# Attention with a relative-position bias, then a mixture of adapters: the bias of half the key tiles moved onto TensorE, the gating onto VectorE, slots and beginning reordered

## The chip, the cores and the metric

The kernel runs on one core of a Trainium2 chip. The metric is the device time of one execution in microseconds. A core has TensorE (PE in the profile; PEld are its weight loads), VectorE (DVE), ScalarE (ACT), GpSimd (POOL), and SyncE (SP), which here only issues DMAs. Each engine works through its own instructions in order and waits on semaphores for the others. PE writes to PSUM alone; DVE and ACT read PSUM.

## What is computed

```python
B, H, S, D = 8, 8, 576, 64                       # q, k, v: (B, H, S, D), float32
scores = q @ k.transpose(0, 1, 3, 2) / sqrt(D)
bias = bias_table[bucket(abs(i - j))]            # 32 buckets, one value per head
attn = softmax(scores + bias)
x = (attn @ v)                                   # as (B * S, H * D) = (4608, 512)

logits = x @ w_gate                              # 8 experts
w = softmax over the two largest logits of a row
out = x + sum over these two of w_e * (x @ A[e]) @ B[e]     # rank 16
```

The bias depends on the distance alone, and from a distance of 128 on it is one value. A value that all keys share cancels in the softmax, so the kernel takes it off the table first: what is left is zero beyond 127.

## The kernel before

**Units and slots.** A unit is one pair of heads of one batch: 32 units, four a batch. A unit has six slots (`SLOTS`). Scores are computed transposed, keys on the partitions and queries along the free dimension. The 512 first keys are four key tiles of 128; their scores are 4 x 576 columns a head, cut in slots of 512 columns: slots 0 to 3 are 2 x 512 columns, slot 4 is 2 x 256. Slot 5 has the 64 last keys (tile 4), the two heads on the two halves of the partitions. In `scores` PE fills one of two score buffers (`sc`, PSUM), and ACT's exp reads it and writes the probabilities in bfloat16: `pm` for the four key tiles (L311), `pe` for the last keys (L319). The two heads stand on partitions 0-63 and 64-127 of `qkT`, so their score matmuls use the two halves of PE's rows.

**Bias.** exp(s + b) = exp(s) exp(b): after the exp DVE multiplies the band of queries within 128 of a key tile by a table of exp(bias) (`bias`): tile 0 in one instruction (512 elements a partition), tiles 1 and 2 together (1536), tile 3 (640), and the last keys (192, L325). The table `eb` is a row of 512 values a head that every partition reads one element further on; the row is computed by DVE and ACT (`table_row`), written to DRAM (`gx_d`), and loaded from there with overlapping rows (`table_load`).

**Values.** In `values` and `whole` PE multiplies the probabilities of a unit by v and a column of ones (L362, 90 matmuls of 65 columns a unit, accumulated in `pv`). This comes one unit later. `normalise` divides by the row sum (L394, L395) and writes `xn`.

**Inputs.** SP loads q, k and v of a batch in pieces of a head, nearly two batches ahead. POOL casts them to bfloat16 (L149, L153), PE transposes q and k (L275), DVE copies them out of PSUM (L279).

**Adapters.** When a batch is done, its tiles of 128 rows are taken in groups of two or three (`Group`): transposes of x, the matmul with A and w_gate together (`zl`), the gates, the product of gate and z (`zt`), its transpose, the matmul with B (`dl`), and the sum with x (L482). A weight softmax over two logits is (1 + tanh)/2. These steps stand in `queue`; `step_pe` takes the next step's PE part, `step_dve` runs what belongs to it on the other engines a little later. `enqueue` interleaves the second half of one group with the first half of the next. z is copied out of PSUM by ACT (L441); of the gates DVE does the maximum and the mask, POOL six small operations and `zt` (L455 to L462), ACT the tanh (L458). The factor 1/2 is in `Bc`, which ACT makes from moe_B (L249) in unit 4. The last batch has a routine of its own (`Last`).

**Order.** The order on each engine is the order of the program: a loop over 192 slots, in which `if s == ...` says what follows the scores of each slot. The PSUM pool `mp` has two buffers (tag `mm`) for everything but scores and `pv`, so a third PE step waits until the first has been copied out. The lines of the slots:

```python
if s == 0: bias(p, 3); finish(p - 1); step_pe()
if s == 1: bias(p, 4); cast_v(u + 1); step_dve(); step_pe()
if s == 2: values(p, 0, 0, 1, 2, 3, 4); cast_qk(u + 2, 0); step_dve()
if s == 3: transpose_pe(u + 1); bias(u, 0); step_pe()
if s == 4: cast_qk(u + 2, 1); transpose_out(u + 1); step_dve()
if s == 5: values(p, 1, 0, 1, 2, 3); bias(u, 1, 2)
```

This is the middle of the kernel; `p` is the unit before `u`, and the last four units (`late`) take values, finish and bias earlier.

Of the kernel before, what the change touches and what calls it, by code (L numbers as in the profile page):

```python
# [33 lines left out]
def kernel(  # L34
# [23 lines left out]
    TE = 192  # L58
# [30 lines left out]
    def load(b):  # L89
# [14 lines left out]

        def tail_qk(*engs):
            for i, (src, eng) in enumerate(zip((q, k), engs)):
                todo.append(lambda i=i, src=src, eng=eng: eng.dma_start(
                    out=qke32[i * 64:(i + 1) * 64],
                    in_=src[b, :, 512:, :].rearrange("h p d -> p h d")))
# [7 lines left out]
        for hp in range(HP if b else 0):  # L117
            main(nc.sync, q32, q, hp)
            main(nc.sync, k32, k, hp)
            if hp == 0:  # L120
                tail_qk(nc.sync, nc.sync)
            main(nc.sync, v32, v, hp)
            if hp == 0:
                tail_v()
        if b == 0:
            main(nc.sync, q32, q, 0)
            main(nc.scalar, k32, k, 0)
            tail_qk(nc.sync, nc.scalar)
            main(nc.sync, q32, q, 1)
            main(nc.sync, k32, k, 1)  # L130
            main(nc.sync, v32, v, 0)
            tail_v()
            todo.append(lambda: table_load(0))
            for hp in range(2, HP + 1):
                if hp < HP:
                    main(nc.sync, q32, q, hp)
                    main(nc.sync, k32, k, hp)
                todo.append(lambda hp=hp: table_load(hp - 1))
                main(nc.sync, v32, v, hp - 1)
        return deque(todo)  # L140
# [26 lines left out]
    nc.sync.dma_start(out=btT, in_=bias_table.rearrange("b h -> h b"))  # L167
    gx = cp.tile([H, GW], FP32, tag="gx")
    gxe = cp.tile([H, GW], BF16, tag="gxe")
    gx_d = nc.dram_tensor("gx_d", (H, GW), BF16, kind="Internal")  # L170
# [3 lines left out]
    ebe = cp.tile([128, HP, TE], BF16, tag="ebe")  # L174

    def table_row():
        nc.vector.memset(gx, 0.0)
# [13 lines left out]
        nc.scalar.activation(gxe, gx, ACT.Exp)  # L191
        nc.scalar.dma_start(out=g, in_=gxe)

    def table_load(hp):
        nc.sync.dma_start(
            out=eb[:, 2 * hp:2 * hp + 2, :],
            in_=bass.AP(tensor=g.tensor, offset=g.offset + 2 * hp * GW,
                        ap=[[1, 128], [GW, 2], [1, TW]]))
        if hp == 0:
            for par in range(2):  # L200
                nc.sync.dma_start(
                    out=ebe[par * 64:(par + 1) * 64, :, :],
                    in_=bass.AP(tensor=g.tensor, offset=g.offset + par * GW + TW - TE,
                                ap=[[1, 64], [2 * GW, HP], [1, TE]]))

# [4 lines left out]
    todo = load(0)  # L210
    for i in range(6):
        todo.popleft()()
    table_row()
    while todo:
        todo.popleft()()
    spread = cp.tile([128, 4, 128, 4], BF16, tag="spread")
    nc.vector.memset(spread, 0.0)
    for c in range(4):
        nc.gpsimd.tensor_copy(out=spread[:, c, :, c], in_=ident)
# [21 lines left out]
    def cast_adapters(i):  # L241
# [4 lines left out]
        elif i == 1:  # L246
            nc.gpsimd.tensor_copy(out=A4[:, :, ER:], in_=Gf)
        else:
            nc.scalar.mul(Bc, Bf, 0.5)  # L249

    def order_adapters(i):
        ps = mp.tile([128, 2, ER + E], FP32, name="Ap", tag="mm")
        for k in range(2):
            for c in range(4):
                lhsT = spread[:, c].rearrange("p m f -> p (m f)")
                nc.tensor.matmul(ps[:, k, :],
                                 lhsT=lhsT[:, (2 * i + k) * 128:(2 * i + k + 1) * 128],
                                 rhs=A4[:, c, :], start=(c == 0 and k == 0), stop=(c == 3),
                                 skip_group_check=True)
        nc.vector.tensor_copy(AW[:, 2 * i:2 * i + 2, :], ps)  # L260
# [15 lines left out]

    def transpose_out(u):
# [9 lines left out]
    def tails_out(b):  # L287
        nc.vector.tensor_copy(batch_tiles(b)[:, :, :, 512:],
                              tps.pop("e").rearrange("p g (i t) -> p g i t", i=2))

    def scores(u, s):
# [7 lines left out]
        if s < SLOTS - 1:  # L299
            c, end = SW * s, min(SW * (s + 1), 4 * S)  # L300
            n = end - c
            while c < end:
                j, q0 = divmod(c, S)
                w = min(S - q0, end - c)
                for h in range(2):
                    rows = slice(h * 64, (h + 1) * 64)
                    nc.tensor.matmul(sc[:, h, c - SW * s:c - SW * s + w],  # L307
                                     lhsT=kT[rows, j * 128:(j + 1) * 128],
                                     rhs=qT[rows, q0:q0 + w], start=True, stop=True)
                c += w  # L310
            nc.scalar.activation(pm[:, :, SW * s:end], sc[:, :, :n], ACT.Exp, scale=scale)  # L311
        else:
            flat = sc.rearrange("p a b -> p (a b)")
            for q0, n in ((0, 512), (512, 64)):
                for h in range(2):
                    rows = slice(h * 64, (h + 1) * 64)
                    nc.tensor.matmul(flat[rows, q0:q0 + n], lhsT=kT[rows, 512:],  # L317
                                     rhs=qT[rows, q0:q0 + n], start=True, stop=True)
            nc.scalar.activation(pe, flat[:, :S], ACT.Exp, scale=scale)  # L319

    def bias(u, j, n=1):
        b, hp = units[u]
        pm, pe = probs[u]
        if j == 4:
            nc.vector.tensor_tensor(pe[:, S - TE:], pe[:, S - TE:],  # L325
                                    _ap(ebe, hp * TE + TE - 1, [[-1, TE]]), op=ALU.mult)
            return
        q0, q1 = max(0, (j - 1) * 128), min(S, (j + 2) * 128)
        e0 = 2 * hp * TW + TW - 1 - (q0 - (j - 1) * 128)
        w = q1 - q0  # L330
        if n == 1:
            t, e = pm[:, :, j * S + q0:j * S + q1], _ap(eb, e0, [[TW, 2], [-1, w]])
        else:
            t = _ap(pm, j * S + q0, [[4 * S, 2], [S + 128, n], [1, w]])
            e = _ap(eb, e0, [[TW, 2], [0, n], [-1, w]])
# [74 lines left out]
    state = {"now": None, "last": None}  # L410
# [385 lines left out]
```

## Time and profile before

| | us |
|---|---|
| three runs | 232.77, 234.53, 236.08 |
| median | 234.53 |
| the profiled execution, whole | 232.95 |
| its span, first to last instruction | 230.8 |

| engine | busy us | share of the span | instructions |
|---|---|---|---|
| PE | 171.1 | 74% | 4138 |
| DVE | 172.0 | 75% | 381 |
| ACT | 173.0 | 75% | 228 |
| POOL | 104.5 | 45% | 202 |

Busy time counts an engine's own instructions; those that only wait, or issue a DMA, are not in it. A group of instructions is shown as: line, engine, operation, out<-in by the program's names, partitions x elements and type, how many | busy time, mean ns of one | idle time of the engine just before them, and what ended most of it. Matmuls overlap, so their mean is longer than the time that each adds. In a view by windows each row is one stretch of the span: its length, then for each engine busy time and number of instructions, the clock that the throttle granted PE, the share of time in which the DMA engines were busy, and GB/s. A line of waits is: who waited <- for whom: us in total, how many times, the longest. A line of the timeline is: start, length, engine, line, operation, names, shape, how many, and in brackets the idle time before it and what ended it.

### The profile page before, as it was taken

The numbers are of one execution on the slowest core, as the hardware profiler recorded it, in microseconds if no ns is written. First come the engines' busy times: TensorE is split into PE (matmuls) and PEld (weight loads), VectorE is DVE, ScalarE is ACT, GpSimd is POOL, SyncE is SP. The second block draws the span as 40 slices with busy tenths as digits, with TensorE's granted clock in tenths as the row PEclk, the third lists the DMA queues.
The fourth block names the chain that finished last, engine by engine and source line by source line (L and its number), as shares of the span: only waits on it lengthen the run. The fifth ranks groups of instructions, "written<-read, shape, count | busy, mean of one in ns | idle before, by whom it ended". The sixth has DMA issues, their size and how long they took to land.

```text
span 230.8 us, 9744 instructions
## 1 busy us (share of the span) xinstructions
PE 171.1 (74%) x4138; PEld 117.4 (51%) x4156; DVE 172.0 (75%) x381; ACT 173.0 (75%) x228; POOL 104.5 (45%) x202
## 2 busy tenths in 40 slices
PE   0477876298586998979578889788879885866741
PEld 0235645175354665646346656566556654653620
DVE  4342577166588889999888899999999978984760
ACT  3186779378679979989598979999889975884422
POOL 1422553630797019296394075666456626312010
PEclk9999999779979999999999999999999999997985
DMA  7989989998886888789889867897779504123106
GB/s 139 177 183 224 215 168 206 223 198 203 196 187 155 181 186 240 161 219 242 212 206 200 188 182 189 189 231 202 193 183 247 171 4 152 47 49 136 48 2 227
DMA packets 123027, 40.18 MB, mean 174 GB/s; under 512 B 116960, under 2 KB 118248, under 8 KB 122984
## 3 DMA queue, kind: packets, MB, share of 16 engines
q1 hardware_dynamic: 121384, 39.16, 70.9%
q8 instruction: 32, 0.52, 1.0%
q10 hardware_dynamic: 1600, 0.40, 0.9%
q14 instruction: 11, 0.09, 0.1%
HBM read 29.84 MB, written 9.45 MB: 170 GB/s over the span
## 4 chain that ended last, share of the span: by engine, by line
DVE 34%; PE 23%; SPq 12%; issue 11%; ACT 9%; DMA 5%; POOL 3%; POOLq 1%; DVEq 0%; ACTq 0%
DVE pm L336 15%; SPq L101 9%; PE pv L362 8%; ACT pm L311 7%; DVE xn L395 7%; PE sc L307 5%; PE tp L275 5%; DVE ot L482 3%; DVE qkT L279 3%; DMA Bf<-in_moe_B_dram 2%; DMA gx_d<-gxe 2%; DVE xT L428 2%; DVE rc L394 1%; PE zl L436 1%; DMA btT<-in_bias_table_dram 1%
## 5 line engine op out<-in xcount | busy, mean ns | idle before, releaser
L311 ACT ACTIVATE pm<-sc 128x1024 bf16<-128x1024 f32 (+1 forms) x160 | 141.3, 939 | 21.2 <-PE sc L307 19.8
L307 PE MATMUL sc<-qkT 64*128 64x384 bf16 (+7 forms) x512 | 61.4, 305 | 23.6 <-ACT pm L311 14.4
L336 DVE TENSOR_TENSOR pm<-pm,eb 128x512 bf16<-128x512 bf16 (+2 forms) x96 | 67.1, 722 | 4.0 <-ACT pm L311 2.2
L362 PEld LDWEIGHTS <-pm 64*128 64x128 bf16 x2480 | 46.7, 96 | 16.8 <-issue 12.8
L362 PE MATMUL pv<-vm,pm 64*128 64x65 bf16 x2480 | 51.0, 194 | 5.4 <-DVE xn L395 3.9
L307 PEld LDWEIGHTS <-qkT 64*128 64x128 bf16 x512 | 20.5, 97 | 38.8 <-issue 30.6
L279 DVE COPY qkT<-tp 128x1024 bf16<-128x1024 bf16 x32 | 22.1, 691 | 22.6 <-PE tp L275 22.0
L455 POOL TENSOR_TENSOR d<-z,top 128x24 f32<-128x24 f32 (+1 forms) x12 | 3.8, 317 | 69.9 <-DVE top L450 61.1
L275 PE MATMUL tp<-ident,qkn 128*128 128x128 bf16 x256 | 22.2, 234 | 8.4 <-DVE qkn L149 6.4
L153 POOL CAST vm<-v 128x512 bf16<-128x512 f32 x32 | 23.6, 736 | 10.3 <-DMA v<-in_v_dram 10.3
L149 POOL CAST qkn<-k 128x512 bf16<-128x512 f32 x32 | 26.7, 834 | 2.9 <-DMA k<-in_k_dram 2.9
L395 DVE TENSOR_TENSOR xn<-pv,rc 128x640 bf16<-128x640 f32 x32 | 26.4, 824 | 1.1
L275 PEld LDWEIGHTS <-qkn 128*128 128x128 bf16 x256 | 15.9, 104 | 16.2 <-DVE qkn L149 6.4
L319 ACT ACTIVATE pe<-sc 128x576 bf16<-128x576 f32 x32 | 20.8, 650 | 4.1 <-PE sc L317 3.6
L317 PE MATMUL sc<-qkT 64*64 64x64 bf16 (+1 forms) x128 | 14.8, 308 | 8.7 <-ACT pm L311 8.5
L149 POOL CAST qkn<-q 128x512 bf16<-128x512 f32 x30 | 19.3, 643 | 2.5 <-DMA q<-in_q_dram 1.4
L482 DVE TENSOR_TENSOR ot<-dl,xn 128x512 f32<-128x512 f32 x28 | 19.2, 685 | 1.0 <-PE dl L478 0.8
L317 PEld LDWEIGHTS <-qkT 64*64 64x64 bf16 x128 | 6.5, 108 | 12.7 <-issue 9.0
L428 DVE COPY xT<-xT_ps 128x1024 bf16<-128x1024 bf16 (+1 forms) x19 | 10.9, 585 | 0.4 <-PE xT_ps L423 0.4
L362 PE MATMUL pv<-ve,pe 64*128 64x65 bf16 x310 | 10.5, 193 | 0.5 <-DVE pe L325 0.5
L458 ACT ACTIVATE th<-df 128x24 f32<-128x24 f32 (+1 forms) x12 | 2.6, 220 | 10.9 <-POOL df L457 10.9
L436 PE MATMUL zl<-AW,xT 128*128 128x136 bf16 x124 | 9.6, 223 | 1.0 <-DVE xT L428 1.0
(94 smaller groups left out, 163.9 us busy)
## 6 DMA issues: line engine op xcount, KB each, us to landing
q<-in_q_dram SPq DMA_DIRECT2D x64, 128.0 KB, 3.4
v<-in_v_dram SPq DMA_DIRECT2D x64, 128.0 KB, 3.9
k<-in_k_dram SPq DMA_DIRECT2D x62, 128.0 KB, 3.7
out_dram<-ot SPq DMA_DIRECT2D x28, 256.0 KB, 3.0
qke<-in_q_dram SPq DMA_DIRECT2D x8, 128.0 KB, 4.0
ve<-in_v_dram SPq DMA_DIRECT2D x16, 64.0 KB, 3.5
out_dram<-otL SPq DMA_DIRECT2D x4, 256.0 KB, 2.4
qke<-in_k_dram SPq DMA_DIRECT2D x7, 128.0 KB, 3.8
```

The costliest lines, as they stand in the source:

```text
L149: eng(out=nats[u][:, i].rearrange("p j (h d) -> p j h d", h=2), in_=src)
L153: eng(out=vals[b % 2][0][:, :, 2 * hp:2 * hp + 2, :D], in_=staged[b][2][:, :, 2 * hp:2 * hp + 2, :])
L275: nc.tensor.transpose(ps[:, i, j, :], nats[u][:, i, j, :], ident)
L279: nc.vector.tensor_copy(batch_tiles(b)[:, hp, :, :512], tps.pop(u).rearrange("p i j t -> p i (j t)"))
L307: nc.tensor.matmul(sc[:, h, c - SW * s:c - SW * s + w], lhsT=kT[rows, j * 128:(j + 1) * 128], rhs=qT[rows, q0:q0 + w], start=True, stop=True)
L311: nc.scalar.activation(pm[:, :, SW * s:end], sc[:, :, :n], ACT.Exp, scale=scale)
L317: nc.tensor.matmul(flat[rows, q0:q0 + n], lhsT=kT[rows, 512:], rhs=qT[rows, q0:q0 + n], start=True, stop=True)
L319: nc.scalar.activation(pe, flat[:, :S], ACT.Exp, scale=scale)
L336: nc.vector.tensor_tensor(t, t, e, op=ALU.mult)
L362: nc.tensor.matmul(pv[:, h, t * W:(t + 1) * W], lhsT=lhsT, rhs=rhs, start=(j == 0 and t == 0 and not cross), stop=(j == 3 and cross == 1), ...
L395: nc.vector.tensor_tensor(_ap(xs[b], hp * 128, [[D, 2], [Dm, 5], [1, D]]), _ap(pv, 0, [[512, 2], [W, 5], [1, D]]), _ap(rc, 0, [[5, 2], [1, ...
L482: nc.vector.tensor_tensor(ot, self.dl, self.x[t], op=ALU.add)
```

## The change

Key tiles 2 and 3 and the last keys get their bias on PE, before the exp: after a score matmul, `near` adds a matmul onto the same columns of the score buffer, whose weights are a reversed identity of 64 rows (`turn`) and whose other operand is a row of 8 x bias from the table `tb`, over 64 keys at a time. (Unit 0 keeps tile 2 on DVE.) Tiles 0 and 1 stay on DVE, each in an instruction of its own.

```diff
+    def near(hp, k0, out, q0, q1, cols, h):
+        a, e = max(q0, k0 - 127), min(q1, k0 + 191)
+        if a < e:
+            rows = slice(h * 64, (h + 1) * 64)
+            nc.tensor.matmul(out(a, e), lhsT=turn[rows, cols],
+                             rhs=tb[rows, hp, a - k0 + 127:e - k0 + 127],
+                             start=False, stop=True, skip_group_check=True)
...
                     nc.tensor.matmul(sc[:, h, o + q0:o + q0 + w],
                                      lhsT=kT[rows, j * 128:(j + 1) * 128],
                                      rhs=qT[rows, q0:q0 + w], start=True, stop=True,
+                                     skip_group_check=True)
+                if j >= (2 if u else 3):
+                    for half in range(2):
+                        for h in range(2):
+                            near(hp, j * 128 + half * 64,
+                                 lambda a, e, h=h: sc[:, h, o + a:o + e], q0, q0 + w,
+                                 slice(0, 128) if half else slice(64, 192), h)
...
+                for h in range(2):
+                    rows = slice(h * 64, (h + 1) * 64)
+                    near(hp, 512, lambda a, e, rows=rows: flat[rows, a:e], q0, q0 + n,
+                         slice(64, 128), h)
```

`near` makes 18 matmuls a unit, in pairs of the two heads, of 255 and 191 columns (slot 2), 63, 127 and 63 (slot 3), 255 and 255 (slot 4), 127 and 64 (slot 5).

The gates: z is copied by DVE, the small operations are DVE's in fewer instructions, POOL keeps `zt`, the tanh is a step of its own, and the factor 1/2 moves from `Bc` to the copy of the transposed `zt`. The groups' steps follow each other without interleaving.

```diff
-        def z_copy(self):
-            nc.scalar.copy(self.z, self.zl)
...
+        def logits(self):
+            nc.vector.tensor_copy(z, self.zl)
...
+            for t in range(n):
+                nc.vector.max(top[:, t, :], lg[:, t, :])
+            nc.vector.tensor_tensor(mid, top[:, :, 0], top[:, :, 1], op=ALU.add)
+            nc.vector.scalar_tensor_tensor(self.df, lg, 2.0, mid.to_broadcast((128, n, E)),
+                                           op0=ALU.mult, op1=ALU.subtract)
+            nc.vector.tensor_tensor(self.mk, lg, top[:, :, 1].to_broadcast((128, n, E)),
+                                    op=ALU.is_ge)
+        def tanh(self):
+            nc.scalar.activation(self.th, self.df, ACT.Tanh, scale=0.5)
+        def gates(self):
+            nc.vector.scalar_tensor_tensor(gate, self.th, 1.0, self.mk, op0=ALU.add, op1=ALU.mult)
...
+            nc.gpsimd.tensor_tensor(
+                self.zt, self.z[:, :, :ER].rearrange("p n (e r) -> p n e r", e=E),
+                gate.to_broadcast((128, n, E, r)), op=ALU.mult)
...
+            s += [(lambda: self.zl_pe(0, self.n), self.logits), (self.tanh, self.gates),
+                  (self.zT_pe, self.zT_out)]
+            return s + [(lambda t=t: self.dl_pe(t), lambda t=t: self.dl_out(t))
+                        for t in range(self.n)]
```

The slots, in the same short form as above (`early` is the first four units, `late` now the last seven):

```diff
+if s == 0: step_dve(); step_pe()
+if s == 1: values(p, 0, 0, 1, 2, 3, 4); step_dve(); cast_v(u)
+if s == 2: bias(u, 0); step_pe(); cast_qk(u + 2, 0)
+if s == 3: bias(u, 1); step_dve(); transpose_pe(u + 1); late: step_pe()
+if s == 4: values(p, 1, 0, 1, 2, 3); transpose_out(u + 1); step_dve(); cast_qk(u + 2, 1)
+if s == 5: finish(p); step_pe()
```

Unit 0's three biases and its values are run in unit 1. The tails of the next batch (transposes and copy) are both in slot 2.

The beginning: the load of bias_table and four pieces of the first k are on ACT's queue; the tables of unit 0 are copied from SBUF (`first_tables`), the others come over DRAM; the first q and k are transposed and copied in parts; the spread identity for the adapters' weights is made in unit 1 and not at the start. The order of SP's loads of batch 0:

```diff
+        main(nc.sync, q32, q, 0)
+        first_k(0, 4)
+        tail_qk(nc.sync, nc.sync)
+        main(nc.sync, q32, q, 1)
+        main(nc.sync, k32, k, 1)
+        todo.append(first_tables)
+        main(nc.sync, v32, v, 0)
+        tail_v()
+        main(nc.sync, q32, q, 2)
+        main(nc.sync, k32, k, 2)
+        todo.append(lambda: table_load(1))
+        todo.append(near_load)
...
```

`first_tables` is four DMAs, `near_load` two. The adapters' weights are loaded in units 2 and 3 (before: unit 1); POOL casts A and w_gate in slot 3 of unit 3 and moe_B in slot 3 of unit 5 (before: ACT, unit 4). Putting A in order on PE is four steps of the queue, from unit 4 on (before: two blocks of eight matmuls in unit 5).

In `Last`, DVE copies only the logits out of PSUM, ACT the rest of two tiles, and `zt` of three tiles reads PSUM. The last unit's biases of tile 3 and of the last keys are no longer behind the loop.

## The prediction

> **What bounds the kernel now.** I read the windows first, cut where the exp that closes a head pair (L319) ends: start, units 1-3, 4-7, 8-27, 28-31, tail. A unit is one head pair of one batch, six slots.
>
> ```profile
> core 0: us, PE busy (x) PEld busy (x) DVE busy (x) ACT busy (x) POOL busy (x), PEclk, DMA share, GB/s
> 0.00:16.43 16.43, 6.53 (x42) 3.10 (x43) 6.54 (x27) 6.93 (x8) 4.79 (x19) 1.00 0.90 165
> 16.43:36.49 20.06, 16.00 (x360) 10.92 (x358) 11.12 (x22) 15.05 (x18) 8.89 (x14) 1.00 0.95 203
> 36.49:66.92 30.43, 21.36 (x516) 14.52 (x513) 17.05 (x39) 21.21 (x28) 14.95 (x28) 0.83 0.91 201
> 66.92:183.46 116.54, 96.97 (x2605) 67.72 (x2608) 105.88 (x222) 103.81 (x136) 64.44 (x116) 1.00 0.81 199
> 183.46:214.25 30.79, 22.66 (x532) 15.64 (x535) 24.11 (x54) 21.30 (x32) 10.45 (x26) 0.94 0.23 82
> 214.25:230.80 16.55, 7.58 (x105) 5.49 (x105) 7.34 (x23) 4.72 (x10) 0.99 (x1) 0.78 0.29 97
> ```
>
> A unit takes 6.7 us in units 1-3, 7.6 in 4-7, 5.83 in 8-27 and 7.7 in 28-31; the middle is the pace that the others miss. There ACT (89%), DVE (91%) and PE (83%) are nearly level, so I asked for the waits of ACT and of PE in that window:
>
> ```profile
> ACT pm L311 <- PE sc L307: 5.6, 20, 0.5
> ACT th L458 <- POOL df L457: 5.1, 6, 2.2
> ```
> ```profile
> PE sc L317 <- ACT pm L311: 7.1, 14, 1.2
> PE sc L307 <- ACT pm L311: 4.8, 12, 0.9
> PE sc L307 <- ACT pe L319: 2.7, 3, 2.2
> ```
>
> ACT is idle 12.7 us in 20 units, 5.1 of them in front of the tanh; PE waits 14.6 us for an exp to free a score buffer. So ACT paces the middle, and DVE is busy beside it. The chain of waits names DVE first (34%), but through many short pieces that sit between PE and ACT. Outside the middle one stall stands out in ACT's timeline, the scaling of moe_B, which waits for its load in the middle of the exps:
>
> ```profile
> 36.77 3.77 ACT L311 ACTIVATE pm<-sc 128x1024 bf16<-128x1024 f32 x4 [0.28 <-PE sc L307]
> 44.52 0.63 ACT L249 ACTIVATE Bc<-Bf 128x512 bf16<-128x512 f32 x1 [3.98 <-DMA Bf<-in_moe_B_dram]
> ```
>
> The prices of the edits are in the groups by form:
>
> ```profile
> L336 DVE TENSOR_TENSOR pm<-pm,eb 128x1536 bf16<-128x1536 bf16 x32 | 33.1, 1033 | 0.7 <-ACT pm L311 0.4
> L336 DVE TENSOR_TENSOR pm<-pm,eb 128x640 bf16<-128x640 bf16 x32 | 20.9, 654 | 0.4 <-ACT pm L311 0.4
> L325 DVE TENSOR_TENSOR pe<-pe,ebe 128x192 bf16<-128x192 bf16 x32 | 8.7, 273 | 0.3 <-ACT pe L319 0.2
> L441 ACT COPY z<-zl 128x408 f32<-128x408 f32 x7 | 3.5, 497 | 1.1 <-PE zl L436 1.1
> ```
>
> **Bias off DVE.** Per unit the 1536, 640 and 192 forms go (1.033 + 0.654 + 0.273 = 1.96 us) and a 768 form comes; between the 512 form (0.477) and the 1536 form it is an estimated 0.62. DVE saves 1.34 x 32 = 43 us. DVE does not pace the middle, so by itself I value this at little: PE's waits there for DVE's xn, pe and the like are 3.6 us in all, of which I take 2.
>
> **Gating on VectorE.** ACT loses the z copies: six of 0.497 and two of 0.38 in the middle, 3.8 us, and their 0.5 of waiting. The tanh now stands a step after the logits, so its 5.1 us of waiting for POOL should go, as should 0.8 of exps that wait for a DVE bias. Middle: -10.2 us. DVE gains a z copy (0.58, from the tail's L591), a mid (0.17), a df and a gate (0.20 each) per group: 11 groups, 12.4 us, hidden in the 43. What is late next is the new queue: a group's steps follow each other with no other group's step between them. After the tanh come gate, POOL's zt (0.84) and the handoffs, an estimated 1.5 us, and PE's next step is the transpose of zt. Everything behind it on PE, the next scores above all, waits. Three steps a unit and eight a group put tanh in slots 2, 0 and 5 in turn. From 2 to 5 it fits; from 0 to 2 some 0.4 us is lost; from 5 to the next 0 there is one slot (0.95 us) and scores have to wait an estimated 1.2. Per eight units 1.6, in the middle (2.5 such turns) +4. Bounds: 0, and 7.5 groups x 1.5 = 11.
>
> **Bias on PE.** A unit gets 18 matmuls in 9 pairs (the two heads), 1400 columns a head, in slots 2 to 5, between scores and exp. Do the heads run side by side? Four score matmuls of the last slot (2 x 512, 2 x 64 columns) take 0.43 us in all, one of 64 columns 0.19: so 576 columns a head stream in 0.24 us, 0.417 ns a column, both heads at once. The new pairs have the same rows: 1400 x 0.417 = 0.58 us a unit. That the second matmul adds to what the first just wrote seems free: twelve zl matmuls, in fours onto the same columns, take 0.89, some 60 ns each for 136 columns. Cover is PE's waiting for ACT, 14.6 / 20 = 0.73 us a unit, but slots 4 and 5 have the short exps (0.60, 0.65) and half the new columns. Bounds 0 and 0.58; I take the middle, 0.3, or +6 in the 20 units. If the cover were gone it would be 12.
>
> Eight transposes of 128 columns, each with its own weight load, take 0.62 us, of which the last one's 0.22 is latency: 57 ns from one to the next. The Trainium skill, "TensorE: Matmul & The Clock Gate", section "Back-to-back issue gap", speaks against this part: in a lasting stream of weight loads and matmuls it gives some 81 ns for each of 128 columns. By that the 18 would be an estimated 1.46 us a unit, 47 us in all, and the kernel slower. The sum goes by the rows.
>
> Middle in all: -10.2 - 2 + 6 + 4 = -2.2 us.
>
> **Units 4-7.** Bc goes to POOL and the load long before it: 3.98 + 0.63 off ACT, -4.6; the tanh of this window (1.9) and the z copy with its wait (0.5 + 0.7): -3.1. What was behind that wait were the exps of unit 4, and the score buffers behind those, so the gain is whole unless loads take its place: DMA is 91% busy here, but k of unit 8 lands at 49 us and is first needed two units later. The bias pairs cost 4 x 0.3. The granted clock is 0.83 in this window and 1.00 after it; with no stall I expect it to stay up, worth an estimated 1 us. Sum -7.5 (bounds -9 and -4). On POOL the cast of moe_B (0.61 us, like its other 512 casts) stands before k of unit 7; POOL is 55% busy in the middle and loses the small gating operations, so this and the adapters' loads, which pass unit 5's and 6's on SP, are put at nothing, and at 0.6 without that cover.
>
> **Units 28-31.** Tanh waits 3.9, z waits 0.8 and copies 1.2 go: -5.9. Bias pairs +1.2; the extra step in slot 3 puts zt's transpose right behind tanh twice, +2.6. The extra step starts three units earlier, so fewer pile up: -1. Sum -3 (bounds -6, +2).
>
> **The beginning.** Spread copies (1.34 us of POOL at 6.2) move to unit 1, k comes in four pieces on ACT's queue, bias_table's load moves from SP to ACT. The first exp was at 10.09; the k cast, transposes and copies now end some 2 us sooner. But the table for unit 1 is the 22nd and 23rd DMA on SP; the 20th was issued at 13.80 before, so about 15, and eb, issued then, landed 4.9 later (DVE waited for it until 18.68). So tb is there at about 20, PE waits for it in slot 2 of unit 1, in order, with the values matmuls behind it; before, that exp began at 20.07. The 2 us are given back. Until 29 us PE is at half speed whatever PEclk says (40 value matmuls take 1.28 to 1.33 us against 0.77 later), so the pairs cost 1.2 a unit there for one or two units: bounds 0 and 3.5, beside a table that might come 2 to 3 us sooner. I take +1 for all before unit 4 (-3, +4).
>
> **Tail.** The last unit's DVE biases (0.48 + 0.25) go; PE's whole-tile matmuls had the head transposes before them anyway. The two z copies shrink. -0.3 (0 to -1).
>
> **Sum.** +1 - 7.5 - 2.2 - 3 - 0.3 = -12 us: span 218.8. The profiled execution took 232.95 us, 2.15 outside its span of 230.8, and is 0.7% under the median of 234.53. So 221.
>
> **Rivals.** (a) *The gain is larger, 203 to 215.* The pairs hide whole (+0), zt comes in time: middle -12, beginning -2, units 28-31 -6, 4-7 -9: -29, 204 at the end. For it: units of 5.27 us, from one L319 to the next, exist in the middle (PE busy 4.98). Against: ACT alone needs 5.0 there. (b) *Little changes, 229 to 238.* The stall of Bc goes, but loads take over: DMA share is 0.95 in units 1-3, and POOL's casts for units 4, 5, 7 and 8 begin within 0.2 us of the landing. Then units 4-7 give 4 and the rest 0. Against: from unit 9 on every load lands 3 us or more ahead of its cast. (c) *Slower, about 251.* PE becomes the bound: 96.97 / 20 = 4.85 us busy a unit, plus 0.58, plus two more changes between 64-row and 128-row matmuls (0.1 each) is 5.63. If PE can't be busier than the 83% it is now, since it waits in order, a unit takes 6.8: +30 over 32 units, less the 12 that the other stages gain. It decides once PE's share stays under about 91%. Against: the 5.27 us units have PE at 94%.
>
> **Chances.** Forecast (215 to 229) 0.51, (a) 0.20, (b) 0.17, (c) 0.12. About 2% is what a measurement can tell from no change. Faster: forecast and (a), 0.71; same 0.17; slower 0.12. The range 209 to 236 leaves out the far end of (a) and (c).
>
> **What would show it.** Right: no ACT wait at Bc; units 4-7 at about 5.9 us; ACT waits for PE's scores up by about 0.3 us a unit in slots 4 and 5; a PE wait for POOL's zt in one group of three; a PE wait for tb near 18 us; DVE busy near 142 us. Wrong: pairs that start one after the other or cost more than 0.6 us a unit; PE over 91% with units above 6 us; casts waiting for loads after 40 us.

## The result and the profile after

The changed kernel is slower: 248.54 us (248.33 to 249.83, four runs) against 234.12 for the kernel before beside it; ratio 1.062 (95% interval 1.054 to 1.071). The forecast was 221, the range 209 to 236. The profiled execution took 248.42 us, its span is 246.6: 15.8 more than the 230.8 of before. Some kernels further on have runs over 1.5% above their own fastest run (three of four of n_none, seven of twelve of best1); their medians are given, but no reading rests on them.

The windows, cut as before at the end of the exp that closes a unit (now L394), with unit 4 in a row of its own:

```profile
core 0: us, PE busy (x) PEld busy (x) DVE busy (x) ACT busy (x) POOL busy (x), PEclk, DMA share, GB/s
0.00:24.41 24.41, 7.53 (x52) 3.61 (x53) 6.49 (x29) 7.82 (x11) 6.06 (x21) 1.00 0.89 122
24.41:43.27 18.86, 15.54 (x412) 11.74 (x412) 9.05 (x18) 15.08 (x19) 6.59 (x12) 1.00 0.87 185
43.27:62.18 18.91, 7.52 (x151) 5.36 (x151) 3.87 (x9) 5.35 (x7) 8.40 (x17) 0.64 1.15 215
62.18:79.38 17.20, 16.04 (x444) 12.16 (x445) 12.69 (x32) 15.33 (x21) 7.98 (x14) 1.00 0.81 189
79.38:201.07 121.69, 109.17 (x2964) 82.30 (x2973) 91.04 (x209) 102.45 (x127) 44.84 (x71) 0.99 0.78 191
201.07:228.01 26.94, 21.47 (x583) 15.58 (x585) 19.38 (x52) 20.93 (x27) 6.97 (x11) 1.00 0.17 54
228.01:246.60 18.59, 8.73 (x110) 6.27 (x111) 6.84 (x22) 4.83 (x9) 0.62 (x1) 0.74 0.29 100
```

| stage | before | after | difference | forecast |
|---|---|---|---|---|
| start to the end of unit 0 | 16.43 | 24.41 | +8.0 | |
| units 1 to 3 | 20.06 | 18.86 | -1.2 | both: +1 |
| unit 4 | 9.69 | 18.91 | +9.2 | |
| units 5 to 7 | 20.74 | 17.20 | -3.5 | 4 to 7: -7.5 |
| units 8 to 27 | 116.54 | 121.69 | +5.2 | -2.2 |
| units 28 to 31 | 30.79 | 26.94 | -3.9 | -3 |
| tail | 16.55 | 18.59 | +2.0 | -0.3 |

Two stages, the start and unit 4, hold 17.2 us of loss. In the timeline, the start shows the first (start, length, engine, line; in brackets the idle time before it):

```profile
6.62 1.20 SPq L213 DMA_DIRECT2D eb<-gxe  x2
7.92 5.17 SPq L217 DMA_DIRECT2D tb<-gxe  x2
13.14 3.47 SPq L101 DMA_DIRECT2D v<-in_v_dram  x2
18.16 0.21 PE L349 MATMUL sc<-tb,turn 64*128 64x63 bf16 x1 [6.22 <-DMA tb<-gxe]
19.57 1.51 ACT L381 ACTIVATE pm<-sc 128x1024 bf16<-128x1024 f32 x2 [7.37 <-PE sc L349]
21.32 0.40 POOL L173 CAST ve<-ve 128x256 bf16<-128x256 f32 x1 [13.30 <-DMA ve<-in_v_dram]
```

The four DMAs of `first_tables` hold SP for 6.4 us (two a line, L213 and L217), the loads behind them come late, and PE waits 6.2 us for the first table with the exps behind it. The list of DMA issues gives KB each and the median us from issue to landing, first over DRAM, then out of one SBUF row:

```profile
eb<-gx_d SPq DMA_DIRECT2D x3, 192.0 KB, 4.1
tb<-gx_d SPq DMA_DIRECT2D x2, 120.0 KB, 3.9
eb<-gxe SPq DMA_DIRECT2D x2, 96.0 KB, 9.3
tb<-gxe SPq DMA_DIRECT2D x2, 40.0 KB, 10.0
```

Half of the bytes (`eb`) take 2.3 times as long, and a third of them (`tb`) 2.6 times. Unit 4 shows the second stall:

```profile
49.39 0.51 SPq L275 DMA_DIRECT2D Af<-in_moe_A_dram  x1
53.45 1.01 POOL L285 CAST A<-Af 128x128 bf16<-128x128 f32 x4 [12.32 <-DMA Af<-in_moe_A_dram]
54.66 0.61 PE L295 MATMUL Ap<-A,spread 128*128 128x136 bf16 x4 [11.42 <-POOL A L287]
55.86 1.02 ACT L381 ACTIVATE pm<-sc 128x1024 bf16<-128x1024 f32 x1 [11.50 <-PE sc L370]
```

SP works through loads without a pause and comes to moe_A at 49.39; the program has it in unit 2. In the kernel before it stood in unit 1 and was issued at 34.86. POOL's cast of A stands in unit 3, PE's ordering of it in unit 4; both engines work in order, and they wait 12.3 and 11.4 us. There is no ACT wait for moe_B any more.

The waits of ACT, then of PE, in units 8 to 27 (total, times, longest):

```profile
ACT pe L394 <- PE sc L349: 9.1, 20, 0.5
ACT pm L381 <- PE sc L349: 4.3, 10, 1.0
ACT pm L381 <- PE sc L370: 4.3, 7, 1.2
```
```profile
PE zT_ps L537 <- POOL zt L530: 5.9, 5, 1.6
PE sc L370 <- DVE zT L542: 1.4, 2, 0.7
PE sc L370 <- ACT pe L394: 1.2, 4, 0.5
PE sc L370 <- ACT pm L381: 0.9, 4, 0.3
```

The roles have changed. Before, PE waited 14.6 us for exps; now that is 2.1 (1.2 + 0.9), ACT waits 17.7 for scores, and PE is busy 90% of the time. The tanh waits are gone, and a wait of PE for `zt` has come.

### The profile page after: what moved, and what is told of

Its sections match the earlier page's. It is cut to its first block, busy times and chain, and to the rows that moved or that the text cites. A ratio compares the mean times of both kernels' runs of the same rounds, so it can differ in the third digit from the quotient of the medians.

```text
span 246.6 us, 10786 instructions
## 1 busy us (share of the span) xinstructions
PE 186.0 (75%) x4709; PEld 137.0 (56%) x4724; DVE 149.4 (61%) x366; ACT 171.8 (70%) x216; POOL 81.5 (33%) x145
## 4 chain that ended last, share of the span: by engine, by line
issue 21%; PE 15%; POOL 12%; SPq 8%; DVE 6%; ACT 4%; DMA 4%; POOLq 0%; ACTq 0%
SPq L101 7%; POOL qkn L163 6%; DMA v<-in_v_dram 4%; PE sc L370 3%; PE pv L427 3%; POOL vm L167 3%; ACT pm L381 2%; POOL zt L530 2%; PE tp L314 2%; PE sc L349 2%; DVE xn L460 1%; DVE pm L401 1%; DVE ot L550 1%; PE zT_ps L537 1%; DVE xT L493 1%
## 5 line engine op out<-in xcount | busy, mean ns | idle before, releaser
L370 PE MATMUL sc<-qkT 64*128 64x384 bf16 (+7 forms) x512 | 63.9, 301 | 10.3 <-ACT pm L381 3.3
L349 PE MATMUL sc<-tb,turn 64*128 64x63 bf16 (+1 forms) x568 | 47.7, 236 | 7.2 <-DMA tb<-gxe 7.2
L401 DVE TENSOR_TENSOR pm<-pm,eb 128x768 bf16<-128x768 bf16 (+1 forms) x65 | 35.9, 561 | 11.3 <-ACT pm L381 11.1
L530 POOL TENSOR_TENSOR zt<-z,gate 128x384 bf16<-128x384 f32 (+1 forms) x11 | 9.2, 840 | 100.6 <-DVE gate L528 100.6
L370 PEld LDWEIGHTS <-qkT 64*128 64x128 bf16 x512 | 22.6, 96 | 26.3 <-issue 15.9
L349 PEld LDWEIGHTS <-turn 64*128 64x128 bf16 (+1 forms) x568 | 29.7, 101 | 9.1 <-issue 6.9
L394 ACT ACTIVATE pe<-sc 128x576 bf16<-128x576 f32 x32 | 20.8, 651 | 17.7 <-PE sc L349 17.1
L163 POOL CAST qkn<-k 128x512 bf16<-128x512 f32 x31 | 21.7, 699 | 1.5 <-DMA k<-in_k_dram 1.4
L167 POOL CAST vm<-v 128x512 bf16<-128x512 f32 x32 | 20.8, 653 | 3.3 <-DMA v<-in_v_dram 3.3
L314 PE MATMUL tp<-ident,qkn 128*128 128x128 bf16 x248 | 19.9, 224 | 2.1 <-POOL qkn L163 1.6
L459 DVE RECIPROCAL rc<-pv 128x10 f32<-128x10 f32 x32 | 7.0, 220 | 10.4 <-PE pv L427 7.4
L537 PE MATMUL zT_ps<-ident,zt 128*128 128x128 bf16 x31 | 3.6, 223 | 10.0 <-POOL zt L530 10.0
```

Of the source, the lines that this page charges most:

```text
L163: eng(out=nats[u][:, i].rearrange("p j (h d) -> p j h d", h=2), in_=src)
L167: eng(out=vals[b % 2][0][:, :, 2 * hp:2 * hp + 2, :D], in_=staged[b][2][:, :, 2 * hp:2 * hp + 2, :])
L314: nc.tensor.transpose(ps[:, i, j, :], nats[u][:, i, j, :], ident)
L349: nc.tensor.matmul(out(a, e), lhsT=turn[rows, cols], rhs=tb[rows, hp, a - k0 + 127:e - k0 + 127], start=False, stop=True, skip_group_check ...
L370: nc.tensor.matmul(sc[:, h, o + q0:o + q0 + w], lhsT=kT[rows, j * 128:(j + 1) * 128], rhs=qT[rows, q0:q0 + w], start=True, stop=True, skip ...
L401: nc.vector.tensor_tensor(t, t, e, op=ALU.mult)
```

## The experiments

Theory 1: the loss is the two DMA stalls, and the rest of the change is about neutral. Theory 2: the bias matmuls make PE the bound, and the stalls only show a time that would be lost elsewhere. Each ratio is to runs of the kernel before that were taken beside it; their median was 233.4 to 234.0 each time.

**The two stalls, one at a time and both.** a_adapt moves the loads, a_table takes unit 0's tables over DRAM (`near_load` then loads all four head pairs), a_both has both edits:

```diff
-        if u == 2 and s < 2 or u == 3 and s == 2:
+        if u == 1 and s < 3:
             load_adapters(s)
```
```diff
-        todo.append(first_tables)
...
+        todo.append(near_load)
         main(nc.sync, k32, k, 2)
+        todo.append(lambda: table_load(0))
         todo.append(lambda: table_load(1))
-        todo.append(near_load)
```

> After, with the three loads of the adapters' weights back in unit 1, slots 0 to 2 (the change had them in units 2 and 3). Theory 1 (two DMA stalls make the loss): the 12.3 us wait of POOL for moe_A in unit 4 goes, PE's 11.4 us wait for A4 with it; units 4 to 7 fall from 36.1 to about 27, the whole from 248.5 to about 239 (236 to 242). Theory 2 (the bias matmuls make PE the bound, and the stall only collects a backlog that would cost elsewhere): under 4 us of gain, 245 or more.

> After, with unit 0's tables taken over DRAM like the others, not copied from one SBUF row a head. Theory 1: the tables land about 4 us after their issue and not 9 to 10; the end of unit 0 falls from 24.4 to 17 to 20, the whole to about 243 (240 to 246). Rival: the start is held by the full queue of loads and not by where the tables come from; then tables and v land as late as before and the time stays within 2 us of 248.5.

> Both edits. Theory 1: the gains add, about 233 (230 to 236), the time of the kernel before: the rest of the change is then worth nothing or little, with the middle (units 8 to 27) still at 121 to 122 us against 116.5. Theory 2: 240 or more.

Measured: a_adapt 242.92 (ratio 1.041, 1.034 to 1.047), a_table 240.58 (1.033, 1.026 to 1.040), a_both 235.79 (1.012, 1.007 to 1.017). Together 12.75 of the 14.4 us between the medians, as theory 1 has it; a_adapt alone gave 5.6, less than it said (its 242.92 lies above the range), a_table 8.0, more than the 5.5 it named. With the tables over DRAM they land 4.0 and 4.4 us after their issue and unit 0 ends at 18.5. The windows from 10 to 16 us, the first of the changed kernel, the second of a_both, show the one SBUF row at work (last columns: DMA share, GB/s):

```profile
10.00:16.00 6.00, 1.26 (x10) 0.51 (x7) 0.00 (x0) 1.94 (x2) 0.00 (x0) 1.00 0.74 25
```
```profile
10.00:16.00 6.00, 2.23 (x18) 0.93 (x14) 0.00 (x0) 2.46 (x3) 2.07 (x4) 1.00 1.11 193
```

The DMA engines were busy 74% of the time and moved 25 GB/s. The Trainium skill, "SBUF — State Buffer", section "Door 1: The DMA port swizzle", says that DMA bandwidth depends on how many of SBUF's 16 ports the partitions reach, and gives some 27 GB/s for one. The 25 GB/s agree with it. Each DMA reads one of the two first rows of one tile; no run read rows that lie further apart, so that the port is the reason is not shown. That the source matters, and not the number of bytes, a_table shows; it also moves these DMAs a few loads back in the queue.

When SP issues the load of A, in the kernel before, a_both, a_table and a_adapt (the changed kernel, above: 49.39):

```profile
34.86 1.40 SPq L234 DMA_DIRECT2D Af<-in_moe_A_dram  x1
35.05 0.51 SPq L275 DMA_DIRECT2D Af<-in_moe_A_dram  x1
41.29 0.51 SPq L275 DMA_DIRECT2D Af<-in_moe_A_dram  x1
43.37 0.51 SPq L275 DMA_DIRECT2D Af<-in_moe_A_dram  x1
```

a_both and a_table differ in the place of the loads alone: it makes 6.2 us. a_table and the changed kernel differ in the tables alone: that makes 8.1. So more than half of the delay of A came from the first stall, which held the same queue, and the two stalls are not independent.

Unit 4 of a_both still takes 12.6 us. The loads of A and of the gate weights land later than POOL asks for them even from unit 1, because the change also asks earlier: PE orders A in unit 4, before it did so in unit 5:

```profile
38.76 1.01 POOL L285 CAST A<-Af 128x128 bf16<-128x128 f32 x4 [6.77 <-DMA Af<-in_moe_A_dram]
40.84 0.21 POOL L287 CAST A<-Gf 128x32 bf16<-128x32 f32 x1 [1.08 <-DMA Gf<-in_moe_w_gate_dram]
41.11 0.61 PE L295 MATMUL Ap<-A,spread 128*128 128x136 bf16 x4 [5.06 <-POOL A L287]
```

**What the Bc stall was worth in the kernel before.** b_bc takes it away there, and nothing else:

```diff
-        if u == 4 and 0 < s < 4:
+        if u == 4 and 0 < s < 3:
             cast_adapters(s - 1)
+        if u == 6 and s == 1:
+            cast_adapters(2)
```

> The kernel before, with the scaling of moe_B (ACT, L249) moved from unit 4, slot 3, to unit 6, slot 1, where its load has long landed. If the prediction's -4.6 us for this wait holds, 229.5 (228 to 231.5). If other waits take its place (loads, the score buffers), 233 to 235.

Measured: 230.79 (0.989, 0.985 to 0.994), inside the first range (228 to 231.5), with a gain of 2.6 and not 4.6. But the trace does not show the reason that was given. Unit 4 fell from 9.69 to 5.23, as foreseen, and unit 5 rose from 6.72 to 11.38: the same wait for A took over.

```profile
38.64 1.01 POOL L244 CAST A<-Af 128x128 bf16<-128x128 f32 x4 [2.09 <-DMA Af<-in_moe_A_dram]
42.10 0.21 POOL L247 CAST A<-Gf 128x32 bf16<-128x32 f32 x1 [1.89 <-DMA Gf<-in_moe_w_gate_dram]
44.01 1.02 ACT L311 ACTIVATE pm<-sc 128x1024 bf16<-128x1024 f32 x1 [3.76 <-PE sc L307]
```

In the profiled run units 4 to 7 take 30.97 us against 30.43 before: of the 4.6 us that the prediction counted whole, nothing is left there, because the Bc wait had covered the loads of A. What is shorter in that run are units 1 to 3 (17.21 against 20.07), which the edit does not touch; where the 2.6 of the medians come from stays open.

**Using A later.** c_order is a_both with the cast and the ordering one unit later:

```diff
-        if u == 3 and s == 3 or u == 5 and s == 3:
-            cast_adapters(u // 4)
-        if u == HP and s == 0:
+        if u == 4 and s == 3 or u == 5 and s == 3:
+            cast_adapters(u - 4)
+        if u == HP + 1 and s == 0:
...
-            if late:
+            if late or 4 < u < 8:
                 step_pe()
```

> Base: both edits (a_both, 235.8 us). Added: POOL's cast of A and w_gate goes from unit 3 to unit 4, slot 3, and PE's ordering of A from unit 4 to unit 5 (with one more step in slot 3 of units 5 to 7, so that from unit 8 on the queue is the same). If the 6.8 us that POOL waits for the two loads is all that is wrong with unit 4, unit 4 falls from 12.6 to about 6.5 and the whole to about 230 (228 to 232). If the loads of q, k and v are as late as the adapters' loads (the queue of SP is full until then), other casts wait in its place and 233 or more is left.

Measured: 231.85 (0.990, 0.986 to 0.995), at the upper end. Unit 4 takes 5.36 in place of 12.63, but unit 7 takes 10.07 in place of 5.71. There the cast of v's last rows waits for its load, `zt` is behind it on POOL, and PE waits for `zt`:

```profile
54.99 0.40 POOL L173 CAST ve<-ve 128x256 bf16<-128x256 f32 x1 [2.37 <-DMA ve<-in_v_dram]
55.36 0.84 POOL L530 TENSOR_TENSOR zt<-z,gate 128x384 bf16<-128x384 f32 x1
56.25 0.34 PE L537 MATMUL zT_ps<-ident,zt 128*128 128x128 bf16 x3 [2.36 <-POOL zt L530]
```

u0_dve asks whether the start is held by the table or by the loads:

```diff
-                if j >= (2 if u else 3):
+                if u and j >= 2:
...
-                for j in range(3):
+                for j in range(4):
                     bias(0, j)
```

(The last keys of unit 0 get their bias on VectorE too, from `eb`.)

> c_order with the whole bias of unit 0 on VectorE (in unit 1), none on PE. PE waits 2.9 us for tb in unit 0 of c_order, with everything of units 0 and 1 behind it. If that is the rest of the beginning's loss, unit 0 ends at 15 to 16 and not at 18.2, and the whole is 229 to 230. If loads of q, k and v set the start then, the gain is gone by unit 3: within 1 us of 231.9.

Measured: 233.10 (0.998, 0.994 to 1.001). Unit 0 ends at 14.98, and unit 3 at 35.94 against 37.01; unit 5 then waits longer for A (1.7 us against 0.5), and unit 7 ends at 64.22 against 64.39. What the start gains is lost in waits for loads by unit 7, and the whole is 1.2 above c_order, not below.

**The middle: what the bias matmuls cost.** n_none is a_both without them, a part of the bias left out of the result:

> a_both without the bias matmuls (568 of them): the bias of key tiles 2 and 3 and of the last keys is left out of the computation. Prediction: they cost 0.3 us a unit, 6 in units 8 to 27, so 115.7 there and about 227 in all. If they lie behind ACT whole: 121 and 235. If PE is the bound and they cost what their columns take (0.58 us a unit and the changes of form): 109 or less, about 218 to 221 in all.

Measured: 229.13 (224.98 to 229.79); its profiled run lost 6 us to a stall in one unit (27), so I read eight undisturbed units, 17 to 24, which hold one whole turn of the adapters' steps. (The fastest of its four runs, 224.98, has no trace.) a_both and c_order take the same 47.9 us there. The windows of these units in the kernel before, c_order, n_none and, further on, best3 and g_only:

```profile
119.84:166.12 46.28, 39.02 (x1043) 27.21 (x1043) 42.98 (x89) 41.53 (x54) 25.02 (x46) 1.00 0.81 197
```
```profile
117.38:165.24 47.86, 44.19 (x1187) 32.38 (x1186) 36.72 (x86) 40.99 (x52) 18.59 (x29) 1.00 0.85 206
```
```profile
113.76:158.28 44.52, 39.78 (x1043) 27.44 (x1042) 36.47 (x86) 40.41 (x51) 19.04 (x30) 1.00 0.82 199
```
```profile
112.25:158.71 46.46, 44.45 (x1187) 32.51 (x1186) 36.19 (x85) 40.74 (x53) 19.05 (x30) 1.00 0.84 203
```
```profile
121.10:175.03 53.93, 42.67 (x1043) 28.03 (x1042) 47.97 (x118) 40.74 (x52) 20.49 (x31) 0.97 0.76 184
```

c_order against n_none: PE is busy 44.19 - 39.78 = 4.41 us more in eight units, 0.55 a unit, which is the 0.58 that the prediction had from the columns. Of it (47.86 - 44.52) / 8 = 0.42 a unit is seen in the time (0.36 over units 10 to 25, the stretch that the expectations further on use); the prediction took 0.3. The rule that the prediction weighed (the Trainium skill, "TensorE: Matmul & The Clock Gate", section "Back-to-back issue gap") would have made 1.46 of it by the prediction's estimate; here the rows were the better guide.

The waits of ACT in units 17 to 24 of n_none:

```profile
ACT pm L381 <- PE sc L370: 2.3, 5, 1.2
ACT pe L394 <- PE sc L387: 1.1, 3, 0.4
```

Even without the bias matmuls ACT stands idle 4.11 of 44.52 us, against 4.75 of 46.28 in the kernel before. The waits for the gating are gone, and 3.4 us of waits for PE's scores stand there, part of them behind `zt` (below); PE is busy 89%, ACT 91%.

**Two guesses at the middle that failed.** m_zt puts `zt` on VectorE (`nc.gpsimd.tensor_tensor` to `nc.vector.tensor_tensor`), m_val moves half of the values matmuls behind the scores of slot 5:

```diff
         if s == 4:
-            if u > 1:
-                values(p, 1, 0, 1, 2, 3)
...
         if s == 5:
-            if u == 1:
-                values(0, 1, 0, 1, 2, 3)
+            if u:
+                values(p, 1, 0, 1, 2, 3)
```

> a_both with the product zt on VectorE and not on GpSimd. PE waits 5.9 us in units 8 to 27 for zt. If PE sets the pace there, about 4 us of it come back and units 8 to 27 take 117 to 119 in place of 121.7, the whole 231 to 233. If ACT sets the pace, as the prediction had it, the exps were not late because of it: within 1 us of 235.8.

> a_both with the second half of the values matmuls (0.77 us of PE) behind the scores of slot 5 and not in front of them, in slot 4. ACT's 9.6 us of waiting in front of the slot-5 exp should go. If that wait is what the middle lost, units 8 to 27 take 113 to 116, the whole about 228 to 231. If PE as a whole is the bound (90% busy), the wait comes back in front of slot 0's exp, and the time stays within 2 us of 235.8.

m_zt measured 234.57 (1.001, 0.997 to 1.005), between its two expectations: PE's wait for `zt` fell only from 5.9 to 4.3 us in units 8 to 27, and a wait for the copy of its transpose rose from 0.8 to 1.6. (The profiled run took 237.50, 3 us over the median, so this reading is a hint.) m_val measured 250.62 (1.073, 1.067 to 1.078), which neither of its expectations had: the 0.45 us in front of slot 5's exp went, and ACT's waits for the plain scores (L370) rose to 8.3 us in units 17 to 24, from 1.9 in the changed kernel. Slots 4 and 5 have ACT's shortest exps; my reading, which no run tries, is that the values in slot 5 pushed the scores of slot 0 behind both.

**The wait for zt.** In a_both the tanh of one group in three stands in slot 5. Unit 16:

```profile
111.61 0.82 DVE L460 TENSOR_TENSOR xn<-pv,rc 128x640 bf16<-128x640 f32 x1
111.84 0.21 ACT L523 ACTIVATE th<-df 128x24 f32<-128x24 f32 x1
112.35 0.17 DVE L528 SCALAR_TENSOR_TENSOR gate<-th,mk 128x24 f32<-128x24 f32 x1
112.60 0.84 POOL L530 TENSOR_TENSOR zt<-z,gate 128x384 bf16<-128x384 f32 x1 [9.17 <-DVE gate L528]
113.50 0.34 PE L537 MATMUL zT_ps<-ident,zt 128*128 128x128 bf16 x3 [1.60 <-POOL zt L530]
```

VectorE gets to `gate` only after `xn`, which slot 5 put in front of it; POOL follows; PE stands 1.6 us with the next scores behind it. The windows of the same trace show what that costs besides (PEclk is the third column from the end):

```profile
110.90:114.30 3.40, 1.49 (x38) 0.88 (x36) 2.01 (x6) 1.82 (x4) 1.70 (x3) 1.00 0.86 201
114.30:117.70 3.40, 3.40 (x65) 2.14 (x58) 2.22 (x3) 2.21 (x3) 3.40 (x6) 0.50 0.79 172
```

A piece of 3.4 us in which PE was busy 44% is followed by one at half clock: unit 16 takes 8.42 us there, and 6.94 in c_order, where the same wait falls across two pieces. z_gap is c_order with a gap:

```diff
+    def zt_next():
+        return bool(queue) and getattr(queue[0][0], "__name__", "") == "zT_pe"
...
         if s == 0:
             step_dve()
-            step_pe()
+            held = zt_next()
+            if not held:
+                step_pe()
...
             step_dve()
+            if held:
+                step_pe()
+                step_dve()
+                held = False
```

(That is slot 1; slot 2 holds the step back likewise until slot 3, units 5 to 7 and the last seven make up for it in slot 4, and slot 5 gets a `step_dve()` before its step.)

> Base: c_order (231.9 us). Added: the step that transposes zt is never taken in the slot right behind the tanh; it waits one slot (in the last seven units the step lost so is made up in slot 4). If PE's waits for zt are what the gating part gave back in place of ACT's tanh waits, then 5.9 us in units 8 to 27, 2.4 (and the half clock behind it) in unit 7 and 3 to 5 behind unit 27 come back for the most part: units 8 to 27 from 120.2 to 114 to 117, the whole 222 to 227. If the wait only moves to the next thing in PE's order, as with zt on VectorE: 230 or more.

Measured: 229.41 (0.985, 0.978 to 0.991), above the 222 to 227 and under the 230 of the other expectation. Its interval overlaps that of c_order, so the gain rests on the units. The waits for `zt` are gone and units 17 to 24 take 46.46 in place of 47.86, 0.18 a unit; but two other waits have grown, 2.4 us of PE for A in unit 5, and in unit 27 VectorE's in front of two output tiles. The profile puts the first down to PE and the second to the store of an earlier tile, which has not left its buffer; with eight buffers (best3, below) both are gone:

```profile
175.24 0.69 DVE L550 TENSOR_TENSOR ot<-dl,xn 128x512 f32<-128x512 f32 x1 [1.97 <-PE sc L349]
177.40 0.69 DVE L550 TENSOR_TENSOR ot<-dl,xn 128x512 f32<-128x512 f32 x1 [1.47 <-DMA out_dram<-ot]
```

best1 is z_gap with u0_dve:

> z_gap and u0_dve together: 220 to 225 if both gains hold and add, under both kernels. If PE's share of busy time is a bound by itself near 90%: 228 or more.

Measured: 231.21 (227.19 to 232.74; 0.989, 0.986 to 0.993). Its five fastest runs, 227.19 to 230.38, lie about z_gap's 229.41: nothing is seen to add, as u0_dve alone would have it, and units 7 and 27 stall in it as well (8.86 and 8.12 us).

best3 takes the two grown waits away:

```diff
-            ot = ms.tile([128, Dm], FP32, name="ot", tag="ot", bufs=4)
+            ot = ms.tile([128, Dm], FP32, name="ot", tag="ot", bufs=8)
...
-                ot = ms.tile([128, Dm], FP32, name="otL", tag="otL", bufs=5)
+                ot = ms.tile([128, Dm], FP32, name="otL", tag="ot", bufs=8)
...
-        if u == 4 and s == 3 or u == 5 and s == 3:
+        if u == 4 and s == 5 or u == 5 and s == 4:
             cast_adapters(u - 4)
-        if u == HP + 1 and s == 0:
+        if u == HP + 1 and s == 1:
```

> z_gap (229.4 us) with two waits taken away that its trace shows: eight buffers for the output tiles, shared by loop and end (VectorE waited 3.4 us in unit 27 for outputs to leave four buffers, and PE's clock halved after it), and the cast of A and its ordering two slots later (PE waited 2.4 us for A in unit 5). If these are stalls of their own: 223 to 226. If a load or PE's order takes their place: 228 or more.

Measured: 224.74 (0.964, 0.958 to 0.971). No unit from 1 on takes more than 7.1 us. This is 9 us under the kernel before and 24 under the change.

**Is the bias on PE worth its cost?** t2_dve (from c_order) and best2 (from best3) put the bias of key tile 2 back on VectorE; t4_dve (from best3) that of the last keys, g_only (from best3) all of it:

```diff
-                if j >= (2 if u else 3):
+                if j >= 3:
...
+            if u:
+                bias(u, 2)
```

(This is t2_dve and best2; the added lines stand in slot 4.)

> c_order with the bias of key tile 2 on VectorE in all units (8 of the 18 bias matmuls of a unit less, one DVE instruction of 0.56 us more). If PE sets the pace and the 18 cost 0.37 us a unit, as the run without them has it, 0.17 us a unit come back: about 227 (225.5 to 228.5). If the prediction's picture holds, in which ACT sets the pace and PE has cover, or if DVE becomes late: 231 or more.

> best3 with the bias of key tile 2 on VectorE. PE is 93% busy in the middle of z_gap, VectorE 78%. If the pace is PE's, 0.17 us a unit come off: 4 to 5 under best3, 219 to 221. With c_order as its base the same edit gave nothing (232.9 against 231.9), where the waits for zt grew to 2.1 us; if VectorE's order is the reason whatever the gap: the same as best3 within 1.5 us.

> best3 with the bias of the last keys on VectorE (4 of the 18 matmuls, all in slot 5; two VectorE instructions of an estimated 0.2 us on 64 partitions more). ACT waits 0.45 us in front of nearly each slot-5 exp. If slot 5 is where PE's bias work hurts, that wait halves: 3 to 5 under best3. If it is PE's total, 191 of 1400 columns are worth 1.5 at most.

> best3 with all bias on VectorE: the gating, the order and the beginning of the change without its first part. VectorE then needs some 1.4 us a unit more (4.5 to 5.9). If it takes over as the bound, units 8 to 27 take 6 us each or more and the whole is 228 to 234, so the bias on PE earns what it costs once the stalls are gone. If PE alone sets the pace, 0.37 us a unit come off and the whole is 213 to 217.

Measured: t2_dve 232.86 (0.998, 0.994 to 1.002), best2 226.23 (0.972, 0.965 to 0.978), t4_dve 234.97 (1.006, 1.002 to 1.010), g_only 248.88 (1.068, 1.060 to 1.075). My expectations of a gain fell. In best2 PE is busy 42.72 in units 17 to 24 and VectorE 39.77, and they take 46.77, where best3 has 44.45, 36.19 and 46.46: PE has 1.7 us less to do and nothing comes of it. So PE's busy time alone does not set the pace.

t4_dve costs 10 us, which neither of its expectations had. Its two instructions take 0.33 us each, not 0.2; they stand in slot 0 ahead of the gating steps, and in units 17 to 24 PE waits 1.7 us for the copy of the transposed `zt` (best3: 0.4). These units take 49.71. Where the rest of the 10 us goes is open.

With all bias on VectorE (the last row of the windows above) it is busy 47.97 of 53.93 us, and ACT waits 9.2 for scores (PE waits for VectorE's copies in turn, 2.3 us for that of the transposed `zt`, 1.7 for that of x). So the first part of the change earns 24 us beside the other parts of it, in the one order of VectorE's work that was tried; t4_dve's 10 us suggest that the order weighs much.

## Why the prediction was wrong, step by step

**The beginning** (+1, bounds -3 and +4; measured +6.8): failed. The first exp did come earlier (8.60 against 10.09), and the wait for unit 1's table was not the trouble. The step that failed: the four DMAs of `first_tables` had no price in the sum at all. No row of before read one SBUF row 64 or 128 times, and so the cost should have stood there with bounds and did not. It was +8.0 at the end of unit 0; a_table gives 5.8 of it back there and 2.5 more in unit 4, where A comes earlier. Some 2 us of the start are left, with PE's wait for the bias table in unit 0 among them (2.9 us in c_order).

**Units 4 to 7** (-7.5; measured +5.7): the wait for moe_B went off ACT, and units 5 to 7 take 5.7 each, as "about 5.9" said. The step that failed is the adapters' loads, "put at nothing, and at 0.6 without that cover". I asked what they delay, units 5's and 6's loads, and not when they themselves arrive and who waits. SP issues loads without a pause until 50 us, so the load of A is issued 14.5 us later (49.39 against 34.86): 6.2 by its move, 8.1 because `first_tables` hold the same queue. The change also orders A a unit earlier, and PE waits for it in order with all scores behind; c_order, which puts that back, takes unit 4 from 12.63 to 5.36. Also "the gain is whole unless loads take its place" went the second way: in the trace of b_bc unit 5 loses what unit 4 gains. Rival (b) named the mechanism and weighed it on the wrong loads.

**The middle** (-2.2; measured +5.2): the bias matmuls' 0.3 a unit was 0.42 in units 17 to 24, 8.3 us for 6 at that rate (0.36, or 7.2, over units 10 to 25). The price of the new queue, +4, was in the right place (slot 5 to slot 0): z_gap gives 0.18 a unit, 3.5 us at that rate, and the half clock behind one such wait is 1.5 more. The step that failed is the relief, -10.2 and -2: by difference it is an estimated 7.9 (the 1.76 us between the windows of before and n_none, in eight units, is 4.4 in twenty, and n_none still has the 3.5 of `zt`). I took ACT's waits away one by one and added them up as if ACT paced alone. n_none shows what stands in their place: ACT is idle nearly as long as before (4.11 us in eight units against 4.75) and waits 3.4 of it for PE's scores, part of that behind `zt`. Whether PE's total (84% busy before, 89% in n_none, 92% in c_order) or the order of its work keeps them late is open: in best2 less work for PE brought nothing.

So rival (c) named the engine that ACT comes to wait for, and was wrong about the price: PE gets to 92% in c_order and 96% in best3, and a unit takes 6.0 and 5.8 us, not 6.8. That its 251 lies near 248.5 is chance; 12.75 us of the loss are the stalls.

**Units 28 to 31** (-3; measured -3.9): held as a sum. Of its terms only that for `zt` was tried: +2.6, and z_gap takes 1.9 off (25.42 against 27.28 in c_order). **Tail** (-0.3; measured +2.0): wrong, and the cause stays open. In the trace a dl step of the queue is left over and runs among the last batch's matmuls; PE waits 0.75 us for its sum on VectorE, and the last tiles' logits are copied out 7.1 us after the last exp's end, not 5.4.

Of what was to be seen: no wait at Bc and PE's wait for `zt` came as written; ACT waits 0.46 us a unit in slot 5 alone, where 0.3 was foreseen for slots 4 and 5; PE's wait for a bias table ended at 18.16 as foreseen, but it was unit 0's table and cost 6.2 us; VectorE was busy 149 us, not 142 (eleven times the gating's 1.15 is also 12.7, not 12.4). Of the signs against, "casts waiting for loads after 40 us" came true; "PE over 91% with units above 6 us" just did not (90% at 6.08 in units 8 to 27).

## What to carry to other kernels

A load that is moved in an in-order queue has to be followed to its own arrival and its first consumer, not only to what it passes; if the queue is behind, its time of issue hangs on everything that holds the queue before it (here 8.1 us of 14.5). Price every new DMA by its source's layout, and where no row shows that layout, put a bound on it and into the range. When several waits of the engine that paces are removed, the sum of the gains can be too high, because the engine comes to wait for another: here ACT for PE, which is busy 44.2 of 47.9 us in c_order and 44.5 of 46.5 in best3.

## What the runs showed of the hardware

DMAs whose source is one SBUF row keep the DMA engines busy (74%) at 25 GB/s, and hold up what is behind them: SP stood 5.17 us at the last two issues and 3.47 at the next two loads.

The granted clock changes in pieces of 3.41 us. In 18 traces of this study, from 30 us on, a piece at full clock was followed by one at half clock 55 times, and in all of them PE had been busy 54% or less; 906 pieces were followed by full clock, all with 49% or more. The Trainium skill, "TensorE: Matmul & The Clock Gate", section "Part 1: The HAM clock gate", has the half rate after an idle window of some 3.4 us. The window agrees; here it need not be idle, half busy is little enough. So a wait of 1.6 us costs up to 1.5 more, or nothing, by where it falls.
